# A scheduler that knows one shared port: a new order of work for an FFT, maxout and SoLU kernel on one Trainium2 core

## The chip, the cores and the metric

The kernel runs on one core of one Trainium2 chip. The core has five engines that work side by side, each through its own list of instructions in order: TensorE (PE, matrix products), VectorE (DVE), ScalarE (ACT), GpSimd (POOL) and SyncE (SP), which here only starts transfers (DMA). SBUF is the on-chip memory that all of them read and write; PSUM is a smaller one in which matrix products land. The metric is device time in microseconds (us), the median of several executions.

## The reference

The program is a two-dimensional FFT of which the real part is kept, then a maxout layer of three branches, then a SoLU layer with a normalisation:

```python
def reference(x, w1, w2, w3, w_out, w_in, w_out2, g_ln):     # x (8, 3072, 256)
    X = np.fft.fft(np.fft.fft(x, axis=1), axis=2).real
    X = X.reshape(8 * 3072, 256)
    a = np.maximum(np.maximum(X @ w1, X @ w2), X @ w3)        # 256 -> 768
    y = a @ w_out                                             # 768 -> 256
    h = y @ w_in                                              # 256 -> 1024
    e = np.exp(h - h.max(-1, keepdims=True))
    solu = h * e / (e.sum(-1, keepdims=True) + 1e-09)
    mu = solu.mean(-1, keepdims=True)
    var = ((solu - mu) ** 2).mean(-1, keepdims=True)
    return ((solu - mu) / np.sqrt(var + 1e-06) * g_ln) @ w_out2   # 1024 -> 256
```

Inputs come as 64-bit floats, the output has 24576 rows.

## The kernel before

**Tiling.** The eight batch blocks are worked through in 48 steps, six per block, each of 512 output rows. The first FFT axis is split in two matrix stages, alpha (once per block) and beta (once per step); the second axis is folded into the weights w1, w2, w3. Values go through PE as pairs of 16-bit numbers, a high part and a low part: a float32 value is cast by ACT to the high part, and GpSimd or DVE subtracts that from the value to get the low part. So for nearly each tile that PE reads there is a GpSimd subtraction ahead of it.

**One step.** Six column chunks (j) with three branches (i). `l1` (L635, PE) makes a branch, with a small beta stage (L530) ahead; ACT (L348) and DVE (L655, L668, L669) finish it; `rl` (L674, DVE) takes the maximum of two branches; `rh` (L678, ACT) and `rlo` (L683, GpSimd) split the result; `m` (L693, PE) multiplies by w_out. `mh` (ACT) and `ml` (L708, GpSimd) split the layer's result `mo`. Then for each of four row tiles `h` (L757, PE), max, exp and scale (L766, L781, L787), `vh` (L814, ACT) and `vl` (L818, GpSimd), a transposing transfer `vt`, and `o` (L832, PE), the product that is written out. Every sixth step, the last of a block, is "special": it has columns of its own, and there the operation of L674 reads two tiles in SBUF, where otherwise one of them lies in PSUM.

**Per block.** x is loaded in four chunks (`xla`, SP), folded by GpSimd (`xgh` L391, `xfly` L433; for block 0 `xgh` is on DVE), squared and split (`xlo` L453, GpSimd, for two chunks of block 0 DVE), and goes into the alpha stage (L471).

**Preparation.** All weights are 64-bit floats in memory. Each is loaded, and DVE turns it into float32 in four instructions (`gd`: L920, L921, L922, L924). The keys are 0, 1, 2 for w3, w1, w2, "o" for w_out, "i" for w_in and "f" for w_out2. Then come a product of the maxout weights with a small DFT matrix `cw` (`t3` and others, L949, L1040), column means of w_out2 (`wfg`, `wfm` L1190, evacuated at L1196), scales by powers of two, and the split in two 16-bit parts (`wil` L1152 for w_in, `wfl` L1220 for w_out2, GpSimd). An operation without instructions, `open` (L1248), comes after all of them; it frees the staging memory for the second layer's tiles, and the first `mh` and so the first `h` depend on it.

**What sets the order.** Nothing of the order is written by hand. Every operation is entered with its engine, a planned duration, the operations it depends on, the buffers it takes and gives, and a due time `vt` (its step, plus a number out of the table `BIAS`, chosen by the operation's name). `Schedule.run` (L250 to L298) then plays through all of them: on each engine it picks, among those that are ready, the one with the smallest pair of (planned start, `vt`), and issues it. So `vt` decides only among operations whose planned start is the same, mostly those that are overdue:

```python
start = max(t, clock[e], *slots)
rank = (max(start, clock[e] + WINDOW[e]), o.vt)
```

`t` is when its inputs are there by plan, `clock[e]` when the engine is free, `slots` when its buffers are. Before, an operation of DVE and one of GpSimd never stand in each other's way in the plan. The order in which the operations are picked is the order of the instructions; synchronisation between engines follows from the data.

Of the kernel before, what the change touches and what calls it, by code (L numbers as in the profile page):

```python
# [37 lines left out]
BIAS = {("xla", 0): 0.924, ("xgh", 0): 24.733, ("xfly", 0): -34.959, ("xsq", 0): 23.794, ("xhi", 0): 18.256,  # L38
        ("xlo", 0): 43.224, ("al", 0): -20.409, ("ah", 0): -7.066, ("alo", 0): -5.301, ("xnm", 0): -16.397,
        ("et", 0): 10.126, ("eth", 0): 11.602, ("etl", 0): -1.123, ("xall", 0): -57.851, ("xsc", 0): -81.962,  # L40
        ("mu", 0): 35.938, "me": -11.444, ("xla", 1): 43.853, ("xgh", 1): -9.882, ("xfly", 1): 12.887,
        ("xsq", 1): 35.589, ("xnm", 1): 32.13, ("xhi", 1): 5.917, ("xlo", 1): -2.706, ("al", 1): 24.31,
        ("ah", 1): 55.437, ("alo", 1): -1.992, ("et", 1): -13.139, ("eth", 1): 18.708, ("etl", 1): -53.13,
        ("xall", 1): -9.436, ("xsc", 1): 2.727, ("mu", 1): -25.808, "xla": -22.81, "xgh": 14.031, "xfly": 106.202,
        "xsq": 141.101, "xnm": 50.062, "xhi": -125.469, "xlo": -81.762, "al": -51.099, "ah": -51.867, "alo": -83.921,
        "et": 0.82, "eth": -4.092, "etl": 0.528, "xall": -54.121, "xsc": -112.086, "mu": 57.404, ("zt", 0): -213.614,
# [20 lines left out]
        ("hf", 47): -63.857, ("os", 47): -15.846, ("const",): -15.666, ("eye",): 16.242, ("constb",): 36.614,  # L67
        ("ld", 0): -17.433, ("ga", 0): 38.059, ("gd", 0): 30.168, ("ld", 1): -15.261, ("ga", 1): -13.662,
        ("gd", 1): 59.201, ("ld", 2): 4.852, ("ga", 2): 6.298, ("gd", 2): -5.654, ("sub", 1): 13.65, ("wc", 1): -40.109,
        ("wce", 1): 17.154, ("am", 1): 20.687, ("wcn", 1): -31.697, ("wne", 1): -17.143, ("wz", 1): 2.591,  # L70
        ("sub", 2): 22.562, ("wc", 2): 39.057, ("wce", 2): 28.715, ("am", 2): -4.123, ("wcn", 2): -24.335,
        ("wne", 2): 37.237, ("wz", 2): -1.79, ("amj",): -17.563, ("ws", "dg"): -46.074, ("ws", "all"): 62.73,
        ("ws", "pow"): 28.767, ("wsc", "part"): 27.98, ("wsc",): 0.287, ("whi", 1): 12.259, ("wlo", 1): -20.428,
# [6 lines left out]
        ("os3", "pow"): 5.53, ("scm", "part"): 47.065, ("scm",): 14.959, ("w3r",): -22.549, ("onm", 0): 11.885,  # L80
        ("ohi", 0): -28.778, ("olo", 0): -3.288, ("onm", 1): -28.401, ("ohi", 1): 25.284, ("olo", 1): -42.867,
        ("w3h",): -49.383, ("w3l",): 23.3, ("ld", "i"): -22.156, ("ga", "i"): 10.736, ("gd", "i"): -26.392,
        ("ami", 0): 19.079, ("wio", 0): 30.795, ("wih", 0): 30.94, ("wil", 0): -27.978, ("ami", 1): -4.217,
        ("wio", 1): 7.182, ("wih", 1): -22.224, ("wil", 1): -6.045, ("amij",): 7.196, ("is", "dg"): 68.428,
        ("is", "all"): 17.003, ("is", "pow"): -4.68, ("isc",): -28.442, ("win",): -7.163, ("gl",): -42.898,
# [5 lines left out]
        ("wf",): 18.981, ("open",): -14.816}  # L91
WINDOW = dict(PE=0, DVE=0, ACT=270, Pool=140, SP=470)
SAME = dict(PE=0, DVE=127, ACT=143, Pool=115, SP=0)


def _trig(num, den):
    num = np.asarray(num) % den
# [1193 lines left out]
```

## Time and profile before

| | us |
|---|---|
| median of three runs | 2072.81 (2070.89 to 2076.14) |
| span of the profiled execution | 2071.3 |
| PE busy in it | 1967.6 (95%) |
| DVE busy | 1731.4 (84%) |
| ACT busy | 1487.6 (72%) |
| POOL busy | 1355.7 (65%) |

The profiled execution's span lies within the range of the three runs, 1.5 us under their median. "Busy" counts an instruction from its start to its end, also when it stands still in between because another engine keeps it from memory. The rows further down are of five kinds: a table by stage (busy time per engine), groups of instructions by line (their sum, the mean of one in ns, and the idle time before them with what ended it), waits of an engine, and a timeline (start, duration, engine, line, operation, tiles; in brackets the idle time just before it and who ended that).

### The profile page before, as it was taken

Reading aid. Unit: us, or ns where it says so; the run is one execution under the profiler, and the core shown is the slowest. Engines: PE = TensorE matmul, PEld = TensorE weight load, DVE = VectorE, ACT = ScalarE, POOL = GpSimd, SP = SyncE. Lnnn points to the kernel's source line nnn. Section 1 sums busy time; section 2 is a strip of 40 time slices with the busy share of each in tenths; the row PEclk is TensorE's granted clock in tenths of the full one; section 3 lists DMA queues with packets and bytes.
Section 4 is the critical chain, followed back from the end, with each engine's and each line's share of the span. In section 5 each row is a group of like instructions: output and inputs, shape, how many; then the busy total and the mean of one; then the engine's idle time right before and its main releaser. Section 6 shows DMA issues by size and latency. Waiting matters only on the chain.

```text
span 2071.3 us, 41047 instructions
## 1 busy us (share of the span) xinstructions
PE 1967.6 (95%) x14892; PEld 1339.3 (65%) x14892; DVE 1731.4 (84%) x3894; ACT 1487.6 (72%) x2933; POOL 1355.7 (65%) x1630
## 2 busy tenths in 40 slices
PE   4659999999999999999999999999999999999998
PEld 2535676666666766666666766676667666666666
DVE  6688889888898879888798888888888888888884
ACT  3668866787668866797677876787667766767765
POOL 4479965696657956597566956576555655655663
PEclk8769999999999999999999999999999999999999
DMA  6624533363344533345334633333433333333335
GB/s 212 154 77 92 120 69 73 60 139 79 67 79 95 113 77 67 83 95 111 72 67 78 118 77 72 72 73 72 82 58 82 72 72 67 72 72 77 62 62 112
DMA packets 472701, 178.82 MB, mean 86 GB/s; under 512 B 453577, under 2 KB 453802, under 8 KB 469290
## 3 DMA queue, kind: packets, MB, share of 16 engines
q1 hardware_dynamic: 472498, 176.20, 40.7%
q8 instruction: 116, 1.90, 0.4%
q14 instruction: 87, 0.71, 0.1%
HBM read 37.75 MB, written 25.17 MB: 30 GB/s over the span
## 4 chain that ended last, share of the span: by engine, by line
PE 73%; DVE 12%; ACT 7%; issue 4%; POOL 2%; DMA 1%; SPq 0%; DVEq 0%; ACTq 0%; POOLq 0%
PE omm L832 19%; PE h L757 19%; PE l L635 17%; PE m L693 15%; DVE l L655 2%; DVE sv L674 2%; DVE v L787 1%; PE beta L530 1%; DVE hst L766 1%; PE alpha L471 1%; ACT jk L792 1%; ACT bs L348 1%; DVE sv L669 1%; ACT e L781 1%; ACT rhl L678 1%
## 5 line engine op out<-in xcount | busy, mean ns | idle before, releaser
L832 PE MATMUL omm<-wf,vt 128*128 128x256 f16 x4608 | 535.2, 273 | 4.7 <-DMA vt<-vh 4.7
L757 PE MATMUL h<-win,mo 128*128 128x512 f16 x2280 | 523.5, 379 | 6.0 <-DVE v L787 4.8
L683 POOL TENSOR_TENSOR rhl<-sv,rhl 128x512 f16<-128x512 f32 x288 | 334.8, 1167 | 269.8 <-ACT rhl L678 258.3
L832 PEld LDWEIGHTS <-vt 128*128 128x128 f16 x4608 | 451.2, 98 | 82.1 <-DMA vt<-vh 5.6
L635 PE MATMUL l<-pq,wl 128*128 128x256 f16 (+2 forms) x3456 | 447.9, 273 | 37.6 <-DVE sv L669 20.5
L818 POOL TENSOR_TENSOR vh<-v,vh 128x1024 f16<-128x1024 f32 x188 | 402.5, 2141 | 73.4 <-ACT vh L814 69.7
L655 DVE SCALAR_TENSOR_TENSOR l<-ny,wn,l 128x256 f32<-128x256 f32 (+1 forms) x672 | 316.7, 482 | 131.8 <-ACT bs L348 129.9
L635 PEld LDWEIGHTS <-wl 128*128 128x128 f16 x3456 | 328.9, 97 | 141.1 <-DVE sv L669 30.6
L693 PE MATMUL m<-rhl,wo 128*128 128x512 f16 x1728 | 417.0, 381 | 1.8 <-POOL wo L1098 1.3
L348 ACT ACTIVATE bs<-l 128x256 f32<-128x256 f32 (+1 forms) x672 | 246.6, 379 | 197.9 <-PE l L635 185.0
L757 PEld LDWEIGHTS <-mo 128*128 128x128 f16 x2304 | 222.9, 98 | 247.9 <-DVE v L787 9.8
L792 ACT ACTIVATE jk<-v,hst 128x1024 f16<-128x1024 f32 x192 | 220.4, 1148 | 96.5 <-DVE v L787 96.2
L766 DVE TENSOR_REDUCE hst<-h 128x1 f32<-128x1024 f32 x190 | 231.2, 1217 | 61.5 <-PE h L757 60.8
L787 DVE SCALAR_TENSOR_TENSOR v<-h,hst,e 128x1024 f32<-128x1024 f32 x190 | 243.2, 1280 | 40.3 <-ACT e L781 31.4
L693 PEld LDWEIGHTS <-wo 128*128 128x128 f16 x1728 | 163.7, 98 | 156.7 <-issue 2.7
L678 ACT CAST rhl<-sv 128x512 f16<-128x512 f32 x288 | 176.2, 613 | 81.1 <-DVE sv L674 59.5
L781 ACT ACTIVATE e<-h,hst,xb 128x1024 f32<-128x1024 f32 x190 | 228.9, 1205 | 6.3
L814 ACT CAST vh<-v 128x1024 f16<-128x1024 f32 x192 | 199.6, 1039 | 2.8 <-DMA vt<-vh 2.8
L674 DVE SCALAR_TENSOR_TENSOR sv<-l,sv 128x512 f32<-128x512 f32 x240 | 164.5, 685 | 2.4
L805 POOL TENSOR_SCALAR hst<-hst,sc 128x1 f32<-128x1 f32 x192 | 66.3, 345 | 139.9 <-ACT jk L792 131.5
L708 POOL TENSOR_TENSOR mo<-s,mw 128x512 f16<-128x512 f32 x96 | 121.7, 1276 | 32.7 <-ACT mw L348 31.9
L668 DVE SCALAR_TENSOR_TENSOR sv<-l,bs 128x256 f32<-128x256 f32 x288 | 120.2, 418 | 8.7 <-POOL bs L647 1.6
(153 smaller groups left out, 2342.5 us busy)
## 6 DMA issues: line engine op xcount, KB each, us to landing
xs<-in_x_dram SPq DMA_DIRECT2D x32, 768.0 KB, 5.5
out_dram<-ob SPq DMA_DIRECT2D x96, 256.0 KB, 2.0
raw<-in_w_dram SPq DMA_DIRECT2D x6, 768.0 KB, 7.4
raw<-in_w_out_dram SPq DMA_DIRECT2D x14, 256.0 KB, 2.9
vt<-vh SPq DMA_TRANSPOSE x192, 4.3
raw<-in_w_in_dram SPq DMA_DIRECT2D x4, 512.0 KB
cb<-in_c_beta_dram SPq DMA_DIRECT2D x1, 1553.0 KB
z<-x SPq DMA_TRANSPOSE x48, 3.5
```

The source lines that it names most:

```text
L348: act.activation(dst, src, AF.Copy, scale=scale)
L635: mm(o, w_[w], hl[:, a, e, c0:c0 + n_], start=(n == 0), stop=(n == 2))
L655: dve.scalar_tensor_tensor(p[:, 0:WA], pq[s][1][:, 0:WA], w, p[:, 0:WA], ALU.mult, ALU.add)
L683: pool.tensor_tensor(t[:, 1], svs.pop((s, j, 0)), t[:, 0], ALU.subtract)
L693: mm(m[:, h], wo[:, w, j, hs], t[:, a], start=(j == 0 and n == 0), stop=(j == NJF - 1 and n == 2))
L757: mm(hp[:, f], m[:, a, d, ts_], win[:, w, d, fs], start=(n == 0), stop=(n == 5))
L766: dve.tensor_reduce(st[:, 0], y["h"], op=ALU.max, axis=AX.XY, negate=True)
L781: act.activation(y["e"], y["h"], AF.Exp, bias=st[:, 11], scale=xbt[s // NSB][:, 12:13], accum_out=st[:, 3])
L787: dve.scalar_tensor_tensor(y["v"], y["h"], st[:, 2], y["e"], ALU.mult, ALU.mult, accum_out=st[:, 4])
L792: act.activation(new(hpool[0], "jk", [128, 2, 512], F16), y["v"], AF.Square, bias=st[:, 4], scale=-float(FF2), accum_out=st[:, 6])
L818: engine.tensor_tensor(y["vh"][:, 1], y["v"].rearrange("p a b -> p (a b)"), y["vh"][:, 0], ALU.subtract)
L832: mm(y["o"][:, 0:D], vt[:, a * 8 + c], wf[:, w, c], start=(n == 0), stop=(n == 23))
```

## The change

The scheduler gets one more rule. Some operations are said to hold a port to SBUF that DVE and GpSimd share: all of GpSimd with a planned duration above 200 ns, and on DVE the four decode instructions, the low-part subtractions, the folding of x, three scale operations, and the maximum of special steps. Such an operation starts, in the plan, no earlier than the last such operation of the other engine ends. Nothing of this is in the program that runs: there is no new wait and no lock in it, and no instruction is added or taken out. The whole `BIAS` table is replaced. Before, its numbers lie within about 230 of zero, now within about 1320; they are on the scale of nanoseconds against the due times of the steps. Two of the some 300 entries are shown. Durations, engines, buffers, and the tables `HOP`, `WINDOW`, `SAME` and `CAPACITY` stay. Lines of the kernel's body move down by 20.

```diff
-        ("wf",): 18.981, ("open",): -14.816}
+        ("wfl", 0): 895.994, ("wfn", 1): -295.076, ("wfh", 1): -1028.944, ("wfl", 1): -145.614, ("wf",): -54.258,
+        ("open",): 1077.592}
...
+PORT = {"gd", "wlo", "w3l", "vl", "xgh", "xlo"}
+
+
+def _holds_port(key, eng, dur):
+    if eng == "Pool":
+        return dur > 200
+    if eng != "DVE":
+        return False
+    if isinstance(key[0], str) and key[0] == "os3":
+        return key[-1] != 0
+    return key[0] in PORT or (key[0] == "rl" and key[1] % NSB == NSB - 1)
...
         self.deps, self.take, self.give, self.lag = list(deps), list(take), list(give), lag
+        self.port = _holds_port(key, eng, dur)
...
         at = {}
+        busy = dict(DVE=0.0, Pool=0.0)
...
                     start = max(t, clock[e], *slots)
+                    if o.port:
+                        start = max(start, busy["Pool" if e == "DVE" else "DVE"])
                     rank = (max(start, clock[e] + WINDOW[e]), o.vt)
...
             clock[o.eng] = end
+            if o.port:
+                busy[o.eng] = end
             o.fn(*o.args)
```

Three places in the order of instructions follow, before and after. Names: `xs`, `uv`, `uh`, `xb` belong to the x of a block, `win` is w_in, `wf` is w_out2, `rhl` the split maximum, `mo` the split result of the maxout layer, `st` a staged weight and `raw` its 64-bit form.

**GpSimd, up to the two `mo` subtractions of step 0**, which are what the first `h` waits for. Before:

```order
L396 MEMSET xb 32x4
L391 TENSOR_TENSOR xs<-xs 96x4x256
L683 TENSOR_TENSOR rhl<-sv,rhl 128x512 x2
L420 TENSOR_SCALAR xb<-xb,sc 128x1 x2
L453 TENSOR_TENSOR uh<-uv,uh 96x1024
L1152 TENSOR_TENSOR win<-st,win 128x512 x2
L683 TENSOR_TENSOR rhl<-sv,rhl 128x512 x2
L1152 TENSOR_TENSOR win<-st,win 128x512 x2
L683 TENSOR_TENSOR rhl<-sv,rhl 128x512
L433 TENSOR_TENSOR uv<-xs 96x512 x2
L708 TENSOR_TENSOR mo<-s_877,mw 128x512
L708 TENSOR_TENSOR mo<-s_976,mw 128x512
```

After:

```order
L440 TENSOR_SCALAR xb<-xb,sc 128x1
L453 TENSOR_TENSOR uv<-xs 97x512 x2
L1240 TENSOR_TENSOR wf<-st,wf 128x1024
L416 MEMSET xb 32x4
L1240 TENSOR_TENSOR wf<-st,wf 128x1024
L703 TENSOR_TENSOR rhl<-sv,rhl 128x512
L411 TENSOR_TENSOR xs<-xs 96x4x256
L703 TENSOR_TENSOR rhl<-sv,rhl 128x512
L453 TENSOR_TENSOR uv<-xs 96x512 x2
L703 TENSOR_TENSOR rhl<-sv,rhl 128x512
L728 TENSOR_TENSOR mo<-s_884,mw 128x512
L728 TENSOR_TENSOR mo<-s_957,mw 128x512
```

Over the whole stretch ahead of these two, sixteen x operations of block 1 have gone behind them (5 of L391, 8 of L433, 3 of L453), with one of L683 and one of L420; none has come ahead of them. The last weight split there is now that of w_out2, before it was that of w_in.

**DVE, around the 128x2 scale operation** (L345, after L365), the place where the second of the two late weights is decoded. Before:

```order
L342 TENSOR_SCALAR am<-am 128x2
L674 SCALAR_TENSOR_TENSOR sv<-l_700,sv 128x512
L920 TENSOR_SCALAR st<-st 128x512
L345 TENSOR_SCALAR am<-am 128x2
L655 SCALAR_TENSOR_TENSOR l_735<-ny,wn,l_735 128x256
L921 TENSOR_SCALAR st<-st 128x512
L979 RECIPROCAL sc<-am 128x1
L922 SCALAR_TENSOR_TENSOR st<-raw,st 128x512
L979 RECIPROCAL sc<-am 128x1
L924 SCALAR_TENSOR_TENSOR st<-raw,st 128x512
L920 TENSOR_SCALAR st<-st 128x512
```

After:

```order
L391 TENSOR_REDUCE am<-spread 128x2
L942 SCALAR_TENSOR_TENSOR st<-raw,st 128x512
L362 TENSOR_SCALAR am<-am 128x2
L371 SCALAR_TENSOR_TENSOR pq<-beta,pq 128x256
L944 SCALAR_TENSOR_TENSOR st<-raw,st 128x512
L365 TENSOR_SCALAR am<-am 128x2
L940 TENSOR_SCALAR st<-st 128x512
L999 RECIPROCAL sc<-am 128x1
L941 TENSOR_SCALAR st<-st 128x512
L999 RECIPROCAL sc<-am 128x1
```

Before, the decode here is that of w_in, between `l1` work of step 0 (`sv`, `l`); after, it is that of w_out2, ahead of that work, and w_in has been decoded earlier.

**SP, the first loads.** `raw` is a 64-bit weight, `xs` a chunk of x, `cw` the DFT matrix, `cal` the alpha matrix, `gl` the gain g_ln. Before:

```order
L878 DMA cal<-in_c_alpha_dram 97x577
L1176 DMA gl<-in_g_ln_dram 128x8x1
L904 DMA raw<-in_w_dram 128x1536 x2
L881 DMA cw<-in_c_w_dram 128x514
L384 DMA xs<-in_x_dram 96x2048
L386 DMA xs<-in_x_last_dram 1x2048
L904 DMA raw<-in_w_dram 128x1536 x2
L384 DMA xs<-in_x_dram 96x2048
L904 DMA raw<-in_w_dram 128x1536
```

After:

```order
L898 DMA cal<-in_c_alpha_dram 97x577
L924 DMA raw<-in_w_dram 128x1536 x2
L404 DMA xs<-in_x_dram 96x2048
L406 DMA xs<-in_x_last_dram 1x2048
L924 DMA raw<-in_w_dram 128x1536 x2
L404 DMA xs<-in_x_dram 96x2048
L1196 DMA gl<-in_g_ln_dram 128x8x1
L901 DMA cw<-in_c_w_dram 128x514
L924 DMA raw<-in_w_dram 128x1536
```

`cw` moved from behind two weight transfers to behind four and two chunks of x.

## Rows read from the trace of the kernel before

**Rows 1.** By stage: us, busy (count) of PE, PEld, DVE, ACT, POOL, clock, DMA, GB/s.

```profile
0.00:170.00 170.00, 95.80 (x585) 64.34 (x586) 124.09 (x222) 97.61 (x185) 97.98 (x71) 0.77 0.49 136
170.00:330.00 160.00, 152.44 (x1132) 101.97 (x1131) 142.00 (x327) 124.03 (x244) 127.97 (x151) 1.00 0.45 95
330.00:2030.00 1700.00, 1685.31 (x12932) 1148.40 (x12931) 1447.99 (x3317) 1245.37 (x2469) 1120.75 (x1391) 1.00 0.40 80
2030.00:2071.30 41.30, 34.02 (x249) 24.62 (x247) 17.31 (x30) 20.56 (x36) 8.98 (x19) 0.95 0.60 120
```

**Rows 2.** Groups of PE, 0 to 170 us: busy, mean ns | idle before, releasers.

```profile
L635 PE MATMUL l<-pq,wl 128*128 128x256 f16 x132 | 20.9, 304 | 25.5 <-DVE sv L669 12.5 <-DVE sv L674 8.6 <-DVE xb L415 2.6
L1040 PE MATMUL prep<-cw,st 128*128 128x256 f32 x24 | 8.6, 520 | 17.1 <-DMA cw<-in_c_w_dram 15.3 <-DVE st L924 1.7
```

**Rows 3.** Groups of DVE, 0 to 170 us: the decode of the weights.

```profile
L920 DVE TENSOR_SCALAR st<-st 128x768 f32<-128x768 f32 (+1 forms) x16 | 16.8, 1053 | 21.7 <-ACT st L916 21.6
L922 DVE SCALAR_TENSOR_TENSOR st<-raw,st 128x768 int32<-128x768 int32 (+1 forms) x16 | 16.3, 1018 | 0.3
L924 DVE SCALAR_TENSOR_TENSOR st<-raw,st 128x768 int32<-128x768 int32 (+1 forms) x16 | 15.7, 980 | 0.3
L921 DVE TENSOR_SCALAR st<-st 128x768 int32<-128x768 int32 (+1 forms) x16 | 12.9, 808 | 0.4
```

**Rows 4.** Timeline of DVE, POOL and PE between 81 and 126 us.

```profile
81.60 0.54 DVE L920 TENSOR_SCALAR st<-st 128x768 f32<-128x768 f32 x1
...
83.76 0.96 DVE L924 SCALAR_TENSOR_TENSOR st<-raw,st 128x768 int32<-128x768 int32 x1
...
110.75 1.83 DVE L920 TENSOR_SCALAR st<-st 128x512 f32<-128x512 f32 x1
...
112.50 3.77 DVE L345 TENSOR_SCALAR am<-am 128x2 int32<-128x2 int32 x1
...
113.91 2.33 POOL L391 TENSOR_TENSOR xs<-xs 96x1024 f32<-96x1024 f32 x1
...
121.00 0.41 DVE L920 TENSOR_SCALAR st<-st 128x512 f32<-128x512 f32 x1
...
122.65 0.68 DVE L924 SCALAR_TENSOR_TENSOR st<-raw,st 128x512 int32<-128x512 int32 x1
...
124.62 1.46 PE L635 MATMUL l<-pq,wl 128*128 128x256 f16 x6 [12.31 <-DVE sv L669]
```

**Rows 5.** Timeline: DFT of the weights, w_out2's chain, and the first h.

```profile
48.99 4.21 PE L949 MATMUL prep<-st,cw 128*128 128x384 f32 x6 [6.25 <-POOL st L943]
...
85.43 0.37 ACT L1196 COPY mean<-prep 128x256 f32<-128x256 f32 x1 [3.95 <-PE prep L1190]
...
108.08 4.21 POOL L1220 TENSOR_TENSOR wf<-st,wf 128x1024 f16<-128x1024 f32 x2 [0.93 <-ACT wf L1216]
...
169.54 1.24 PE L757 MATMUL h<-win,mo 128*128 128x512 f16 x5
```

**Rows 6.** Groups of POOL, 0 to 170 us: the x work.

```profile
L433 POOL TENSOR_TENSOR uv<-xs 96x512 f32<-96x512 f32 (+1 forms) x20 | 27.3, 1385 | 18.6 <-DVE xs L391 18.3
L391 POOL TENSOR_TENSOR xs<-xs 96x1024 f32<-96x1024 f32 (+1 forms) x7 | 16.6, 2377 | 0.7 <-DMA xs<-in_x_dram 0.6
L453 POOL TENSOR_TENSOR uh<-uv,uh 96x1024 f16<-96x1024 f32 (+1 forms) x5 | 11.9, 2375 | 10.9 <-ACT uh L445 7.7 <-DVE st L921 3.2
```

**Rows 7.** Special steps, 330 to 2030 us: a group, one case, PE's waits.

```profile
L674 DVE SCALAR_TENSOR_TENSOR sv<-sw,sv 128x512 f32<-128x512 f32 x43 | 52.4, 1219 | 0.5
...
1272.41 2.13 POOL L818 TENSOR_TENSOR vh<-v,vh 128x1024 f16<-128x1024 f32 x1 [1.41 <-ACT vh L814]
1272.45 2.64 DVE L674 SCALAR_TENSOR_TENSOR sv<-sw,sv 128x512 f32<-128x512 f32 x1
...
PE l L635 <- DVE sv L669: 5.7, 11, 1.7
```

**Rows 8.** Timeline of PE in the last 20 us.

```profile
2060.85 6.81 PE L832 MATMUL omm<-wf,vt 128*128 128x256 f16 x48 [3.28 <-DMA vt<-vh]
```

More of the change, by code (lines that the diff above doesn't have):

```diff
@@ L37 @@
 HOP = dict(PE=200, DVE=130, ACT=150, Pool=150, SP=60)
[L38 to L46, printed above, removed]
[20 rows of a table removed]
[L67 to L73, printed above, removed]
[6 rows of a table removed]
[L80 to L85, printed above, removed]
-        ("ld", "f"): -43.368, ("ga", "f"): 6.612, ("gd", "f"): 10.13, ("wfg", 0): -13.295, ("wfg", 1): -3.645,
-        ("wfg", 2): -9.739, ("wfg", 3): 5.268, ("wfm",): 21.588, ("wfe",): -36.028, ("wfs", 0): 66.321,
-        ("amf", 0): -22.861, ("wfs", 1): -10.945, ("amf", 1): 23.161, ("amfj",): 59.432, ("fs", "dg"): -30.537,
-        ("fs", "all"): 7.01, ("fs", "pow"): -47.813, ("wfc", "part"): 19.001, ("wfc",): -25.835, ("wfn", 0): 18.746,
-        ("wfh", 0): 26.324, ("wfl", 0): 8.648, ("wfn", 1): -13.905, ("wfh", 1): 18.869, ("wfl", 1): -9.387,
-        ("wf",): 18.981, ("open",): -14.816}
@@ new lines @@
+BIAS = {("xla", 0): -329.39, ("xgh", 0): -352.9, ("xfly", 0): -237.583, ("xsq", 0): -435.605, ("xhi", 0): -107.549,
+        ("xlo", 0): -1322.849, ("al", 0): -257.121, ("ah", 0): -372.322, ("alo", 0): -843.063, ("xnm", 0): -438.913,
+        ("et", 0): -26.783, ("eth", 0): -472.589, ("etl", 0): 21.7, ("xall", 0): -231.403, ("xsc", 0): -762.511,
+        ("mu", 0): -263.605, "me": -989.32, ("xla", 1): 812.734, ("xgh", 1): 1087.32, ("xfly", 1): -706.162, ("xsq",
+        1): -784.131, ("xnm", 1): 273.605, ("xhi", 1): -41.517, ("xlo", 1): -296.985, ("al", 1): -59.039, ("ah", 1):
+        23.429, ("alo", 1): -1245.312, ("et", 1): 41.852, ("eth", 1): -787.021, ("etl", 1): -37.623, ("xall", 1):
+        -671.872, ("xsc", 1): 150.998, ("mu", 1): -146.585, "xla": -121.712, "xgh": 860.482, "xfly": 104.414, "xsq":
+        88.716, "xnm": 825.803, "xhi": -264.459, "xlo": -876.228, "al": -887.438, "ah": -103.593, "alo": 758.005,
+        "et": -792.112, "eth": -676.383, "etl": -484.142, "xall": -422.562, "xsc": 925.06, "mu": -227.338, ("zt", 0):
[23 rows of a table added]
+        902.054, ("sub", 1): -353.424, ("wc", 1): -74.322, ("wce", 1): -904.275, ("am", 1): -349.423, ("wcn", 1):
+        -613.95, ("wne", 1): 476.473, ("wz", 1): 607.37, ("sub", 2): 21.812, ("wc", 2): -1099.738, ("wce", 2):
+        -124.669, ("am", 2): -326.155, ("wcn", 2): 1085.624, ("wne", 2): -1047.421, ("wz", 2): -742.007, ("amj",):
+        756.246, ("ws", "dg"): -870.362, ("ws", "all"): -257.833, ("ws", "pow"): 252.253, ("wsc", "part"): 519.632,
+        ("wsc",): 757.111, ("whi", 1): -475.846, ("wlo", 1): -288.588, ("whi", 2): -203.12, ("wlo", 2): 606.608,
[6 rows of a table added]
+        -197.78, ("scm",): -789.692, ("w3r",): -199.777, ("onm", 0): -992.761, ("ohi", 0): -889.296, ("olo", 0):
+        -842.891, ("onm", 1): -281.679, ("ohi", 1): 617.645, ("olo", 1): -203.121, ("w3h",): -904.114, ("w3l",):
+        -251.361, ("ld", "i"): -1239.52, ("ga", "i"): -671.925, ("gd", "i"): -269.314, ("ami", 0): 353.278, ("wio",
+        0): -576.076, ("wih", 0): -996.473, ("wil", 0): -266.625, ("ami", 1): -789.095, ("wio", 1): -368.532, ("wih",
+        1): -890.573, ("wil", 1): 704.53, ("amij",): -109.604, ("is", "dg"): -540.108, ("is", "all"): 6.052, ("is",
+        "pow"): -660.953, ("isc",): 73.116, ("win",): -922.531, ("gl",): -312.41, ("ld", "f"): 151.409, ("ga", "f"):
+        -381.267, ("gd", "f"): -978.057, ("wfg", 0): 1084.436, ("wfg", 1): 16.262, ("wfg", 2): -400.13, ("wfg", 3):
+        -82.377, ("wfm",): 151.873, ("wfe",): -53.124, ("wfs", 0): -519.032, ("amf", 0): 718.226, ("wfs", 1):
+        -908.005, ("amf", 1): -1080.261, ("amfj",): -666.536, ("fs", "dg"): 79.961, ("fs", "all"): 723.361, ("fs",
+        "pow"): -308.223, ("wfc", "part"): 837.499, ("wfc",): -501.014, ("wfn", 0): -290.121, ("wfh", 0): -842.554,
+        ("wfl", 0): 895.994, ("wfn", 1): -295.076, ("wfh", 1): -1028.944, ("wfl", 1): -145.614, ("wf",): -54.258,
+        ("open",): 1077.592}
```

55 rows, old and new, of the table BIAS are left out of this document.

## The prediction

> **What bounds the kernel now.** First the table by stage, for where PE is not at work [rows 1]. Span less busy time of PE is 74.2 us in the first 170 us (170 − 95.8), 7.6 up to 330, 14.7 in the 1700 us after that, and 7.3 in the last 41. In the steady part PE is 99% busy at full clock. The order of work can't shorten PE's own work, so of the 2071.3 us only these 103.8 are at stake, and 74 of them lie ahead of the first `h`, which starts at 169.54 [rows 5].
>
> Second, the groups of PE in that stretch, for what it waits on. Idle ahead of L635 is 25.5 us, 12.5 of it for DVE's `sv` [rows 2], and one wait makes up nearly all of that: 12.31 us at 124.62 [rows 4].
>
> Third, DVE there. The decode of the weights is 64 instructions, together 16.8 + 16.3 + 15.7 + 12.9 = 61.7 us [rows 3]. Undisturbed they take less: a 768-wide one 0.54 us in the first form (L920) and 0.96 in the second (L924), a 512-wide one 0.41 and 0.68 [rows 4]. Each form is two of the four lines and half the weights have each width, so free time would be 8 × (2 × 0.54 + 2 × 0.96) + 8 × (2 × 0.41 + 2 × 0.68) = 24.0 + 17.4 = 41.4 us. That is 20.3 us of stretching. One instruction on two numbers per partition (L345, 112.50) took 3.77 us, where a 512-wide one takes 0.41: at least 3.4 more. So DVE stands still for about 23.7 us here. It does so beside GpSimd's work: the 1.83 us decode of 110.75 lies beside the `wf` split of 108.08 to 112.29 [rows 5], and the 3.77 us one ended at 116.27, 0.03 us after the x fold that GpSimd began at 113.91 [rows 4]. The lock of the change is about this. It exists in the plan alone: what can change is which instructions stand side by side.
>
> **The change part by part.** *Up to the first `h`, what moves behind it.* GpSimd drops 5 of L391, 8 of L433 and 3 of L453 from in front of the two `mo` subtractions: 5 × 2.38 + 8 × 1.39 + 3 × 2.38 = 30.1 us [rows 6], all x work of block 1, not needed before step 6. Nothing new comes ahead. On PE, small pieces of block 1 and of step 1 go behind too, 11 operations and by the same rows' kind about 6.2 us; that is work put off, not saved.
>
> *What is then late.* `open` waits for the last weight. Before, w_in came last: decoded from 110.75 on, its split and the x work on GpSimd then lay in front of `mo`. After, w_in is decoded early and w_out2 comes last. Its chain took from the evacuation of its means at 85.43 to the end of its last split at 112.29, 26.9 us [rows 5]. In the new order its mean product stands behind `l1` of chunk 3 of step 0; counting PE's work and waits in front of it by the trace of before gives an end at 115 to 120 (estimate). Plus 26.9, plus some 4 to 5 for the `mo` split: first `h` at 146 to 152, 18 to 23 us sooner. Less the 6.2 us of PE work put off, PE loses 12 to 17 us fewer. The bounds: nothing gained (the chain through w_out2 is as late as that through w_in was) and 23.7 (all of DVE's standing still). I take **−14**, near the one row that shows such a stall, 12.31.
>
> *The first loads.* `cw` goes behind two more weight transfers and two chunks of x on SP. PE waited 15.3 us for it [rows 2], so `t3` starts 10 to 15 us later. Behind it PE waits 6.25 us for a GpSimd subtraction at 48.99 anyway [rows 5], and only 95.8 of 170 us are work, so it can be caught up; 0 to 2 us, contained in the −14. Uncovered it would cost 15 − 6.25 = 9 us; that keeps the upper end.
>
> *Steps 0 to 5.* The 30.1 us on GpSimd come back. From 170 to 330 it was busy 128.0 of 160 us [rows 1], so 32 us are free, enough in sum. By the order, 22 of the 30 stand in front of the `vl` of the third tile of step 2; by step 4 both orders have the same work behind them. PE then waits when a split comes late. Bounds: −3 (the x work in step 0 was in the way too) and +27.5 (rival C). PE was held up 7.6 us in all in this stretch, with GpSimd 80% busy; I take **+4**, near that row.
>
> *Special steps.* From 330 to 2030 the 43 maxima of L674 with both inputs in SBUF took 52.4 us [rows 7]; another instruction with two 512-wide inputs takes 0.68 [rows 4], so 43 × 0.68 = 29 us of work and 23 us of standing still on DVE, a good part of it hidden: PE waits 5.7 us there for `sv` (11 waits) [rows 7]. Bounds −5.7 and +5.7; the new order keeps these apart by plan, but one case shows how little of the plan need be off: GpSimd began at 1272.41 and DVE at 1272.45, and the maximum took 2.64 us [rows 7]. I take **−3**.
>
> The Trainium skill ("SBUF — State Buffer", sections on the two sides of SBUF and "Who interferes with whom") says that the pair of ports is locked by whichever engine starts first, for that whole instruction, and that the order of issue, not the shape, decides who waits. The case at 1272.41 agrees (0.04 us decide 2 us); the one at 112.50 doesn't quite, since there DVE was issued 1.41 us ahead of the fold and still ended after it. Taken strictly, the rule speaks against this change: a plan can't promise 0.04 us, so special steps would give 0 for −3, and the sum would be 3 us higher.
>
> *The end.* PE waits 3.28 us at 2060.85 for the transposed tile [rows 8]; the new order puts the last product of step 46 and the first of 47 in another sequence, with one more product in front of that place. Bounds −3.3 and +3.3, taken **−2**.
>
> Everything else is the same instructions on the same engines, so it costs nothing, with PE's 99% in the steady part as the cover; if due times there were worse, it would show as PE's idle time above 14.7.
>
> Sum: 2071.3 − 14 + 4 − 3 − 2 = 2056.3 us of span; the median lay 1.5 above the span of before, so **2058**.
>
> **The rivals.** *B, the start gains nothing (the change doesn't do what it says).* Instructions drift by more than 0.04 us against the plan, so the decode of w_out2 meets other GpSimd work, as that of w_in did, and the new last chain takes 18 to 23 us longer than 26.9. For it: it is a chain over DVE, ACT, GpSimd and PE, each step with a hop, and 23.7 us of stretching moved to it are just that gap. Against it: 16 GpSimd instructions that were the partners of the stretch are gone from there. Time: 2071.3 + 0 − 3 − 2 + 1.5 = 2068, with the 5.7 and 3.3 either way 2063 to 2076.
>
> *C, GpSimd's backlog in steps 0 to 2 (slower).* Its idle time of 32 us lies in pieces, behind the casts that it waits for, and can't be filled. If it stays 20% idle with 22 us more to do, the 160 us become (128 + 22) / 0.8 = 187.5: +27.5, PE waiting for `vl` and `rlo`. Time: 2071.3 − 14 + 27.5 − 2 + 1.5 = 2084. It turns the sign from a backlog cost of some 19 us on, that is when GpSimd keeps nearly its whole idle share. Against it: what was moved is only wanted in step 6, and the subtractions in question have due times of their own, ahead of it.
>
> **How the numbers follow.** The main case: 0.64, 2042 to 2067. B: 0.22, 2063 to 2076. C: 0.14, 2077 to 2090. In the main case all at its best would be 2071.3 − 23.7 − 3 − 5.7 − 3.3 + 1.5 = 2037; I leave 0.06 below 2042. With C left out above 2078 (0.13) the range is 2042 to 2078. 0.3% is 6.2 us, about what a measurement of this kernel can tell from no change: faster is below 2066.6, slower above 2079. Faster 0.61 of the main case and 0.06 of B: 0.67. Same: 0.03, 0.16 and 0.01 of C: 0.20. Slower: 0.13.
>
> **What would show it.** In the profile after: first `h` (L777) between 146 and 152 us; PE's idle time up to it about 60 in place of 74; the 64 decodes together nearer 45 than 61.7 us; the wait for `sv` at L655 in the start gone. Between first `h` and step 3, PE's idle time at about 12 in place of 7.6, with GpSimd over 85% busy there. The special maxima at a mean nearer 0.9 than 1.22 us. Wrong would make it: a first `h` behind 160 (B); PE idle over 20 us between first `h` and 330, released by GpSimd (C); `t3` so late that the first beta stage is late with it; or waits at L852 for the transposed tile all through the steady part, since the new due times let some `h` and `o` of one tile come closer together.

## The result

The changed kernel took 2043.13 us (median of four runs, 2041.56 to 2043.93), the kernel before, beside it, 2074.19 (2070.89 to 2076.14). The ratio is 0.9856, with a 95% interval of 0.9842 to 0.9869: some 31 us faster, where 15 were forecast. The time lies within the stated range of 2042 to 2078, 1 us from its lower end. The profiled execution spans 2042.1 us, 29.2 less than that of before.

The table by stage, cut at the first `h`, answers to [rows 1]; columns are us, then busy time and count of PE, PE's weight loads, DVE, ACT and GpSimd, granted clock, DMA share, GB/s:

```profile
0.00:85.00 85.00, 41.41 (x234) 31.19 (x235) 62.94 (x85) 45.04 (x82) 30.69 (x26) 0.80 0.61 177
85.00:142.28 57.28, 43.48 (x256) 28.07 (x255) 44.87 (x118) 40.26 (x84) 37.36 (x29) 0.88 0.35 95
142.28:330.00 187.72, 182.84 (x1408) 123.28 (x1406) 167.87 (x391) 152.25 (x297) 167.89 (x188) 1.00 0.49 108
330.00:2000.00 1670.00, 1656.59 (x12722) 1131.77 (x12721) 1425.49 (x3269) 1226.76 (x2431) 1100.42 (x1368) 1.00 0.40 80
2000.00:2042.10 42.10, 36.21 (x279) 26.75 (x277) 19.16 (x34) 24.05 (x42) 16.24 (x22) 0.99 0.62 126
```

PE's idle time up to the first `h` is now (85 − 41.41) + (57.28 − 43.48) = 57.4 us, before 74.2. Behind it 4.9, 13.4 and 5.9, before 7.6, 14.7 and 7.3 [rows 1]. GpSimd is 89% busy from the first `h` to 330 (before 80%), and PE waits less there, not more.

The 29.2 us in full: idle up to the first `h` −16.8, in the 188 us behind it −2.7, in the steady part −1.3, at the end −1.4, and PE's busy time −7.0 (1967.6 to 1960.5 by the page).

The groups of PE and of DVE up to 170 us answer to [rows 2] and [rows 3]:

```profile
L655 PE MATMUL l<-pq,wl 128*128 128x256 f16 x179 | 26.8, 297 | 10.3 <-DVE sv L694 4.8 <-DVE sv L689 2.7 <-DVE s L689 1.7
L1060 PE MATMUL prep<-cw,st 128*128 128x256 f32 x24 | 8.5, 525 | 28.7 <-DMA cw<-in_c_w_dram 28.5
```

```profile
L944 DVE SCALAR_TENSOR_TENSOR st<-raw,st 128x768 int32<-128x768 int32 (+1 forms) x16 | 16.0, 998 | 0.3
L940 DVE TENSOR_SCALAR st<-st 128x768 f32<-128x768 f32 (+1 forms) x16 | 14.2, 886 | 16.0 <-ACT st L936 15.9
L942 DVE SCALAR_TENSOR_TENSOR st<-raw,st 128x768 int32<-128x768 int32 (+1 forms) x16 | 14.1, 881 | 0.2
L941 DVE TENSOR_SCALAR st<-st 128x768 int32<-128x768 int32 (+1 forms) x16 | 10.2, 639 | 0.3
```

The wait of 12.3 us is gone (the longest for `sv` in the start is now 1.7); the 64 decodes take 54.5 us, before 61.7. Their free time, that is without a neighbour that holds them up, is 41.4 us by the prediction's count. The timeline of DVE (answers to [rows 4]) shows where the 13 us of stretching that are left lie:

```profile
40.33 3.38 DVE L940 TENSOR_SCALAR st<-st 128x768 f32<-128x768 f32 x1
...
55.96 2.05 DVE L940 TENSOR_SCALAR st<-st 128x512 f32<-128x512 f32 x1 [0.23 <-ACT st L936]
58.04 0.43 DVE L941 TENSOR_SCALAR st<-st 128x512 int32<-128x512 int32 x1
58.51 0.69 DVE L942 SCALAR_TENSOR_TENSOR st<-raw,st 128x512 int32<-128x512 int32 x1
```

They lie ahead of 58 us, where GpSimd folds the x of block 0 and subtracts weights, work that is needed there. Behind 58 us nearly all decodes take their free time: of the stretching, 12.6 us lie ahead of 58 us and 0.4 behind, in before 9.2 and 11.0. So what the new order has removed is the stretching of the late weights. And the way to the first `h` (PE and GpSimd, answers to [rows 5]):

```profile
105.79 1.13 PE L1210 MATMUL prep<-st,ones 128*128 128x256 f32 x4 [1.01 <-ACT st L368]
...
129.05 2.13 POOL L1240 TENSOR_TENSOR wf<-st,wf 128x1024 f16<-128x1024 f32 x1 [0.18 <-ACT wf L1236]
131.18 1.15 POOL L703 TENSOR_TENSOR rhl<-sv,rhl 128x512 f16<-128x512 f32 x1
132.29 2.35 POOL L411 TENSOR_TENSOR xs<-xs 96x1024 f32<-96x1024 f32 x1
134.61 1.15 POOL L703 TENSOR_TENSOR rhl<-sv,rhl 128x512 f16<-128x512 f32 x1
135.72 2.50 POOL L453 TENSOR_TENSOR uv<-xs 96x512 f32<-96x512 f32 x2
138.19 1.16 POOL L703 TENSOR_TENSOR rhl<-sv,rhl 128x512 f16<-128x512 f32 x1
139.31 2.49 POOL L728 TENSOR_TENSOR mo<-s,mw 128x512 f16<-128x512 f32 x2
...
142.28 2.75 PE L777 MATMUL h<-win,mo 128*128 128x512 f16 x12
```

The chain through w_out2 is what the prediction named, and GpSimd stands without a gap between its last split and `mo`.

### The profile page after: what moved, and what is told of

Same layout as the page of the kernel before. It is cut to its first block, busy times and chain, and to the rows that moved or that the text cites. A ratio compares the mean times of both kernels' runs of the same rounds, so it can differ in the third digit from the quotient of the medians.

```text
span 2042.1 us, 40722 instructions
## 1 busy us (share of the span) xinstructions
PE 1960.5 (96%) x14892; PEld 1341.1 (66%) x14892; DVE 1720.3 (84%) x3894; ACT 1488.4 (73%) x2933; POOL 1352.6 (66%) x1630
## 4 chain that ended last, share of the span: by engine, by line
PE 66%; DVE 8%; ACT 8%; POOL 5%; issue 3%; DMA 1%; DVEq 0%; POOLq 0%; ACTq 0%
PE h L777 17%; PE omm L852 17%; PE l L655 15%; PE m L713 13%; DVE v L807 2%; ACT jk L812 2%; POOL vh L838 2%; DVE hst L786 1%; ACT e L801 1%; PE beta L550 1%; PE alpha L491 1%; DVE l L675 1%; DVE sv L694 1%; DMA vt<-vh 1%; POOL rhl L703 1%
## 5 line engine op out<-in xcount | busy, mean ns | idle before, releaser
L655 PEld LDWEIGHTS <-wl 128*128 128x128 f16 x3456 | 329.6, 97 | 121.4 <-DVE sv L689 16.8
L713 PEld LDWEIGHTS <-wo 128*128 128x128 f16 x1728 | 168.1, 98 | 164.8 <-issue 3.8
L807 DVE SCALAR_TENSOR_TENSOR v<-h,hst,e 128x1024 f32<-128x1024 f32 x190 | 243.5, 1281 | 29.8 <-ACT e L801 15.3
L859 ACT ACTIVATE ob<-omm,hst 128x256 f32<-128x256 f32 x192 | 89.8, 468 | 69.6 <-PE omm L852 49.4
```

The source lines that it names most:

```text
L655: mm(o, w_[w], hl[:, a, e, c0:c0 + n_], start=(n == 0), stop=(n == 2))
L713: mm(m[:, h], wo[:, w, j, hs], t[:, a], start=(j == 0 and n == 0), stop=(j == NJF - 1 and n == 2))
L807: dve.scalar_tensor_tensor(y["v"], y["h"], st[:, 2], y["e"], ALU.mult, ALU.mult, accum_out=st[:, 4])
```

## The experiments

Theory: the gain lies ahead of the first `h`, and it is GpSimd's work in company with the decode (side by side with it) that was in the way. Rivals: GpSimd's queue alone, that is the x work standing in front of `mo`; the order of the weights; the lock as such, the table as such; and, behind the first `h`, GpSimd's backlog. The edits are shortened: `...` stands for what is left out, and words behind # are remarks. The numbers in one table first. Each ratio is taken against executions of before beside it, whose median lay between 2072.1 and 2074.2. Idle time is PE's, span less busy time by stage: up to the first `h`, in the 187.7 us behind it, from there to 2000, and after. First `h`, idle and busy time are of one execution each. new_start, lock_start_only, old_rest_locked and no_special_lock issue the same instructions in the same order as after up to the first `h`, so their first `h` at 140.5 to 142.3 and their 57.4 to 59.8 us of idle time up to it show how far two executions can lie apart.

| kernel | time, ratio to before (interval) | first h | idle by stage | PE busy |
|---|---|---|---|---|
| before | 2074.19 | 169.5 | 74.2, 7.6, 14.7, 7.3 | 1967.6 |
| after | 2043.13, 0.9856 | 142.3 | 57.4, 4.9, 13.4, 5.9 | 1960.5 |
| lock_old_table | 2102.19, 1.0146 (1.0131 to 1.0161) | 206.5 | 99.0, 3.1, 11.7, 12.4 | 1974.7 |
| new_table_no_lock | 2072.70, 1.0001 (0.9992 to 1.0011) | 168.9 | 73.5, 9.6, 11.4, 9.9 | 1968.6 |
| x_held | 2091.86, 1.0098 (1.0082 to 1.0114) | 150.6 | 62.6, 30.5, 13.6, 8.4 | 1972.8 |
| company_add | 2058.29, 0.9933 (0.9916 to 0.9949) | 157.0 | 73.0, 4.9, 13.5, 6.0 | 1959.8 |
| company_fill | 2048.70, 0.9881 (0.9866 to 0.9895) | 146.1 | 62.7, 4.9, 13.7, 6.1 | 1959.1 |
| cw_first | 2044.32, 0.9859 (0.9845 to 0.9874) | 143.1 | 56.8, 4.9, 13.7, 6.0 | 1962.1 |
| new_start | 2086.77, 1.0063 (1.0048 to 1.0078) | 140.5 | 58.5, 15.3, 32.6, 8.3 | 1968.7 |
| new_rest | 2059.42, 0.9935 (0.9918 to 0.9951) | 168.7 | 73.7, 6.4, 8.7, 6.5 | 1963.1 |
| x_paced | 2098.95, 1.0125 (1.0110 to 1.0140) | 150.3 | 61.8, 8.4, 44.0, 8.5 | 1975.2 |
| lock_start_only | 2049.50, 0.9885 (0.9870 to 0.9899) | 141.4 | 59.8, 7.0, 11.8, 9.4 | 1959.3 |
| old_rest_locked | 2083.89, 1.0052 (1.0037 to 1.0067) | 141.5 | 59.5, 15.0, 26.9, 12.4 | 1971.2 |
| no_special_lock | 2049.50, 0.9887 (0.9870 to 0.9903) | 140.7 | 58.8, 7.1, 12.1, 9.3 | 1959.9 |

**The port, by itself.** Useless GpSimd work is put where GpSimd waits anyway, the order being that of after:

```diff
+    with_company(("xlo", 0, 1), 4)     # pool.tensor_tensor(dum, dum, dum, ALU.add)
+    with_company(("wz", 2), 5)
+    with_company(("w3z",), 4)
```

> The kernel after in its own order, with 13 additions of 896 columns in SBUF put in on GpSimd where it waits anyway (4 behind xlo of chunk 1 of block 0, 5 behind the second wz, 4 behind w3z): about 27 us of work that nobody needs, beside the weight decode. Theory of the port: DVE stands still beside them, the decode and the weight scaling between 57 and 110 us take 8 to 15 us longer, first h 4 to 12 us later than 142.3, time 2047 to 2056. Rival (only GpSimd's queue in front of mo counts): GpSimd was idle there, first h within 2 us, time 2042 to 2046.

It took 15 us more than after and the first `h` came 14.7 us later: the theory's sign, a larger size than its 4 to 12, and nothing of the rival, by which work in GpSimd's idle time costs nothing. DVE beside GpSimd in its timeline:

```profile
58.13 7.84 POOL L1279 TENSOR_TENSOR dum<-dum 128x896 f32<-128x896 f32 x4
...
58.48 1.78 DVE L943 TENSOR_SCALAR st<-st 128x512 int32<-128x512 int32 x1
60.30 2.05 DVE L944 SCALAR_TENSOR_TENSOR st<-raw,st 128x512 int32<-128x512 int32 x1
62.39 2.05 DVE L946 SCALAR_TENSOR_TENSOR st<-raw,st 128x512 int32<-128x512 int32 x1
```

Four additions in 7.84 us, 1.96 each, and beside them each DVE instruction takes about as long (1.78 to 2.05), whatever its free time (0.43 and 0.69 in after at the same place): one addition goes by for one DVE instruction. The decode, all of it:

```profile
L946 DVE SCALAR_TENSOR_TENSOR st<-raw,st 128x768 int32<-128x768 int32 (+1 forms) x16 | 18.7, 1168 | 0.3
L944 DVE SCALAR_TENSOR_TENSOR st<-raw,st 128x768 int32<-128x768 int32 (+1 forms) x16 | 17.6, 1100 | 0.2
L942 DVE TENSOR_SCALAR st<-st 128x768 f32<-128x768 f32 (+1 forms) x16 | 17.3, 1084 | 16.2 <-ACT st L938 16.0
L943 DVE TENSOR_SCALAR st<-st 128x768 int32<-128x768 int32 (+1 forms) x16 | 14.2, 889 | 0.3
```

67.8 us, 13.3 more than after. To tell the port from GpSimd's being busy, fills take the additions' place:

```diff
+    with_company(("xlo", 0, 1), 9)     # pool.memset(dum, 0.0)
+    with_company(("wz", 2), 11)
+    with_company(("w3z",), 9)
```

> As company_add, at the same three places of GpSimd's list, but with 29 fills of 896 columns (0.845 us each in the run with additions, 24.5 us together; the 13 additions took 24.7) that write SBUF and read nothing. If GpSimd's being busy there is what cost the 15 us (its own later work comes late), the time is 2054 to 2060 as with the additions. If it is the port and only GpSimd's reading holds it against DVE operations with two SBUF inputs, the forms with two inputs (L944, L946 lines by after) keep 0.68 and 0.96, and the time is 2043 to 2048; if the fills hold it as well, each DVE operation beside them takes 0.85 and the time lies between, near 2050.

GpSimd was busy as long (29 fills took 26.6 us, 13 additions 24.7), and 5.6 us were lost in place of 15.2. The time lies 0.7 us above the 2043 to 2048 that were expected if only GpSimd's reading counts. Its timeline:

```profile
57.67 8.82 POOL L1279 MEMSET dum<- 128x896 f32 x9
...
58.05 1.03 DVE L943 TENSOR_SCALAR st<-st 128x512 int32<-128x512 int32 x1
59.11 0.69 DVE L944 SCALAR_TENSOR_TENSOR st<-raw,st 128x512 int32<-128x512 int32 x1
59.84 0.69 DVE L946 SCALAR_TENSOR_TENSOR st<-raw,st 128x512 int32<-128x512 int32 x1
```

The forms with two inputs in SBUF keep 0.69 beside fills; the form with one input goes from 0.43 to 1.03. So some 60% of the price of the additions (9.6 of 15.2 us) is due to what GpSimd reads, not to its being busy; and the other 5.6 us aren't all its being busy, since the one-input form is held up by fills too. The Trainium skill ("SBUF — State Buffer", sections "SBUF: two separate sides" and "Who interferes with whom") says of the two-input operations that they meet GpSimd only where it reads SBUF, and of `tensor_scalar`, the one-input form here, that it can run in a mode that takes the shared pair of ports and then contends with GpSimd; the runs agree on both (0.69 and 1.03 us beside fills).

**Lock or table.** First the lock with the table of before:

```diff
-BIAS = {("xla", 0): -329.39, ...          # the new table
+BIAS = {("xla", 0): 0.924, ...            # the table of before
```

> The scheduler's lock with the table of before. In this order 31 x operations (L411, L453 by the after lines) stand ahead of the first mo subtraction on GpSimd, where before has 22 and after 9. Theory (what counts is how much GpSimd work lies in front of and beside the weight decode): first h later than the 169.5 us of before, 172 to 190, and a time of 2073 to 2095. Rival (the lock itself is the gain, the table only trims it): first h near 150 and a time of 2045 to 2060.

The theory's side, worse than its range: first `h` at 206.5, 30 us slower than the before beside it. A plan that reckons with the port is not faster by itself. Then the table without the lock:

```diff
-                    if o.port:
-                        start = max(start, busy["Pool" if e == "DVE" else "DVE"])
```

> The new table without the lock. 11 x operations ahead of the first mo subtraction (after 9). Theory (the order of the start does it, whoever made it): first h at 142 to 150, time 2043 to 2055. Rival (the lock does it): the decode lies beside GpSimd work again, first h at 160 or later, time above 2060.

No change against before, so here the rival was right on the time, but not for its reason. The decode is not stretched more than in after, and DVE waits for what it is to decode:

```profile
L942 DVE SCALAR_TENSOR_TENSOR st<-raw,st 128x768 int32<-128x768 int32 (+1 forms) x16 | 15.0, 939 | 0.3
L940 DVE SCALAR_TENSOR_TENSOR st<-raw,st 128x768 int32<-128x768 int32 (+1 forms) x16 | 15.0, 938 | 0.3
L938 DVE TENSOR_SCALAR st<-st 128x768 f32<-128x768 f32 (+1 forms) x16 | 11.8, 738 | 27.1 <-ACT st L934 27.1
L939 DVE TENSOR_SCALAR st<-st 128x768 int32<-128x768 int32 (+1 forms) x16 | 11.2, 699 | 0.3
```

53.0 us of decode, but 27.1 of waiting (after 16.0), and the last decode ends at 123.7 in place of 105.2: one load of w_in went out at 87.92, after the last of them at 60.00. Few x operations ahead of `mo` are not enough; the loads and decodes have to come in time as well. That the table was chosen for a plan with the lock's starts would explain why it needs them, but that isn't shown. Its numbers aren't nanoseconds: they are added as they are to a due time in steps, which spans only some 50. Of the new table's 255 numbers 238 are over 50 in size (before 78 of 283), so it mostly ranks kinds of operations, whatever their step.

**Is it the moved x work?** The kernel before, with one dependency more:

```diff
-        op(("xgh", *k), ..., v - 0.3, deps=[("xla", *k)])
+        op(("xgh", *k), ..., v - 0.3, deps=[("xla", *k)] + [("ml", 0, 1)] * (b == 1))
```

> The kernel before with one more dependency: the x work of block 1 on GpSimd may start only behind the second mo subtraction of step 0, so that 6 x operations stand ahead of the first mo (before 22). Weight order, table and plan otherwise as before, no lock. Theory: the wait of 12.3 us for sv is gone, the 64 decodes take 50 to 56 us in place of 61.7, first h at 145 to 155, time 2050 to 2060. Rival (the new order of the weights, w_in first and w_out2 last, is the gain): first h at 163 or later and a time of 2066 to 2075.

The first `h` came at 150.6, 19 us sooner, without table, lock or a new order of weights, as the theory had it. Not as the theory had it, the longest wait for `sv` is still 7.0 us and the decode takes 58.9, where 50 to 56 were expected. So company isn't all of it. In before, GpSimd's own list was in the way as well: it is busy for 35.3 of the 37.8 us from 130.33 to the first `mo` subtraction at 168.10, and over half of that is x work of block 1:

```profile
L391 POOL TENSOR_TENSOR xs<-xs 96x1024 f32<-96x1024 f32 (+1 forms) x3 | 7.3, 2419 | 0.1
L453 POOL TENSOR_TENSOR uh<-uv,uh 96x1024 f16<-96x1024 f32 (+1 forms) x3 | 6.4, 2130 | 0.7 <-ACT uh L445 0.7
L433 POOL TENSOR_TENSOR uv<-xs 97x512 f32<-97x512 f32 (+1 forms) x4 | 5.9, 1498 | 0.0
```

company_add and company_fill show that company has a price of its own; x_held takes company and queue away at once, so how the gain of the start divides between them is not shown. The time was 32 us above its range. Everything came back behind the first `h`:

```profile
150.58:330.00 179.42, 150.67 (x1103) 99.76 (x1102) 130.98 (x311) 128.63 (x242) 153.55 (x155) 0.92 0.46 103
```

28.8 us of PE idle time, with GpSimd 86% busy: the size of rival C of the prediction, in another kernel, though only 4.6 us of PE's waits there are ended by GpSimd itself, the most by DVE and ACT. GpSimd's list there has six x instructions between the second `mo` and the first `vl`, and seven more between the first two `vl`. So the chunks were released one step apart (the new end of the line alone):

```diff
+           deps=[("xla", *k)] + [("ml", NSB * (b - 1) + c, 1)] * (b > 0))
```

> The kernel before with the x work of each block spread over the steps of the block ahead: chunk c of block b may be folded only behind the second mo subtraction of step 6(b-1)+c. x_held released four chunks at once behind the first mo and lost 30.5 us of PE idle time in the 187.7 us behind its first h. Theory (that loss is GpSimd's backlog): first h near 150.6 as in x_held, idle time in the 187.7 us behind it at 5 to 12 us, time 2055 to 2068. Rival (it comes from the old order of the weights and of step 0, whatever x does): idle time there above 20 us, time above 2075.

Right on the first `h` (150.3) and on the stretch behind it (8.4 us in place of 30.5), so that loss came of the four chunks released at once. Wrong on the time: PE lost 44.0 us later (some 30 between 290 and 650), waiting for DVE's `sv` and `v` and once 3.2 us for a transposed tile. The dependency makes the scheduler plan all of the rest anew with due times fitted to another flow; which of them fails there wasn't followed.

**The first load.** In after's order, `cw` issued first:

```diff
     const_load()
+    const_load2()
-    pop(("const",), "SP", 750, const_load2, (), -0.85, lag=2000)
+    pop(("const",), "SP", 750, lambda: None, (), -0.85, lag=2000)
```

> The kernel after with the load of cw issued first on SP; all else stays in its order. The DFT products (L1060) can start at about 16 to 20 in place of 28.55 us. Theory (PE has room there, DVE's decode of w1 and w2 and GpSimd set the pace up to 58 us): first h within 2 us of 142.3, time 2041 to 2044. Rival (the 13 us by which the first load came later were a loss): first h 5 to 9 us sooner, time 2034 to 2038.

No gain: the 13 us by which `cw` came later are covered, as the theory had it. The same products of `cw` then wait 28.1 us for other things, 19.0 for DVE's decode and 9.1 for ACT.

**Start and rest apart.** The scheduler switches table and lock once the first `h` is planned (new_rest the other way round):

```diff
-                    if o.port:
+                    if o.port and not begun:
...
+            if k == ("h", 0, 0):
+                begun = True
+                for m in self.ops.values():
+                    m.vt = m.late          # due time by the other table
```

> The scheduler runs with the lock and the new table until the first h has been planned, and from there on with the table of before and without the lock. Theory (the gain lies ahead of the first h): first h at 142 to 143, time 2043 to 2052, special maxima back to a mean of 1.1 to 1.25 us. Rival (the new order in steps 0 to 5 keeps the gain from being given back): PE's idle time from the first h to 330 us over 10 us, time 2055 to 2070.

> The other half: table of before and no lock until the first h has been planned, from there on the new table with the lock. Theory: first h at 169 to 170, special maxima at a mean of 0.75, time 2066 to 2073. Rival (the lock is worth something in the steady part): 2058 to 2065.

Both theories fell; of new_rest, the rival's time of 2058 to 2065 was met. The new start with the old rest is slower than before by 13 us, although its first `h` comes at 140.5. PE's idle time behind it:

```profile
140.48:330.00 189.52, 174.20 (x1271) 113.98 (x1269) 150.95 (x355) 139.03 (x268) 154.01 (x174) 0.97 0.44 89
330.00:2000.00 1670.00, 1637.41 (x12614) 1119.47 (x12612) 1412.87 (x3235) 1214.28 (x2406) 1095.80 (x1333) 1.00 0.40 80
```

15.3 and 32.6 us. And the new rest with the old start saves 14 us, with the first `h` at 168.7. So the two halves don't add: new start alone +13, new rest alone −14, both −31. Behind the new start the new rest is worth 44 us (2086.8 to 2043.1), behind the old one 14. Next, which part of the rest:

```diff
-                    if o.port:
+                    if o.port and not begun:       # lock until the first h, new table all through
```

> The new table all through, the lock only until the first h has been planned. Theory (behind the first h the table's due times carry the gain and the lock moves only DVE's own waiting): first h at 140 to 143, special maxima back at 1.0 to 1.25 us, time 2042 to 2050. Rival (the lock is needed behind the first h as well): PE idle behind the first h above 35 us (24.2 in the kernel after), time 2055 to 2085.

```diff
-                    if o.port and not begun:       # of new_start
+                    if o.port:                     # lock all through, old table behind the first h
```

> New table until the first h has been planned, the old one behind it, the lock all through. new_start, which is the same without the lock behind the first h, took 2086.8 with 56 us of PE idle time behind it. If the lock is what keeps the rest in order, idle time behind the first h falls to 24 to 32 us and the time to 2045 to 2060; if the table is, it stays at 2075 to 2095.

```diff
-    return key[0] in PORT or (key[0] == "rl" and key[1] % NSB == NSB - 1)
+    return key[0] in PORT
```

> The kernel after, but the maximum of special steps isn't said to hold the port; all other holders stay. Theory (what DVE stands still there is mostly hidden): special maxima at a mean of 1.0 to 1.25 us in place of 0.75, PE's idle time from 330 to 2000 up by 0 to 6 us from 13.4, time 2042 to 2050. Rival (these waits are on PE's path): idle time up by over 10 us, time above 2053.

The table is it: with it and no lock behind the first `h` the time is 2049.5, with the lock and the old table 2083.9. The lock saves some 6 us there, about the size that can be told, and all of that by the entry of the special maxima, since without that entry the time is the same 2049.5 and GpSimd's list is the same as without the lock. It isn't saved where most of the maxima are: with the lock PE's idle time in the table's third stretch is 1.6 us more, and 2.1 and 3.5 less in the second and the last (after against lock_start_only). The expected size of those maxima was wrong: 0.78 us in both (41 in 330 to 2000 us), where 1.0 to 1.25 was expected. The table without the lock and the lock without the table each keep them nearly clear of GpSimd, where the maxima of before take 1.22 [rows 7] (new_table_no_lock, then lock_old_table, 330 to 2000 us):

```profile
L692 DVE SCALAR_TENSOR_TENSOR sv<-sw,sv 128x512 f32<-128x512 f32 x39 | 29.3, 752 | 0.4
L693 DVE SCALAR_TENSOR_TENSOR sv<-sw,sv 128x512 f32<-128x512 f32 x42 | 33.2, 789 | 0.4
```

## Why the prediction was right, and where it wasn't

The sign, the place of most of the gain and the mechanism at the start were right; the size was half of what was measured, and the range held by 1 us. Of the 29.2 us, 7.0 are in PE's busy time, for which the prediction had no term, and the near hit of the start is in part luck. By its terms:

- **The start, −14: measured −16.8.** The way there was less exact than the sum. w_out2's mean product ended at 106.9, forecast 115 to 120; its chain took 24.3 us (forecast 26.9); and from its last split to the first `h` it took 11.1 us, forecast 4 to 5, because six GpSimd instructions, three of them x work of block 1, still stood ahead of `mo` (the rows at 131.18 to 138.19). Against the middle of the forecast, 149, the product was put some 10.6 us too late, the chain 2.6 too long and the last piece 6.6 too short; they made 142.3, outside "146 to 152", and that errors of both signs left the term near is luck. The decode got less free than forecast (54.5 us, not near 45), since the remaining stretch is beside block 0's own x work. That GpSimd's company stretches the decode and delays the first `h` is shown (company_add, company_fill); that moving x work behind `mo` is by itself enough for a first `h` some 19 us sooner too (x_held). The prediction named both the x work in front of `mo` and its company with the decode and didn't price them apart; the runs don't either, so how the 16.8 us divide is open.
- **The first loads, 0 to 2 with 9 uncovered: nothing.** PE waited 28.5 us in place of 15.3 for `cw`, and cw_first gained nothing.
- **Steps 0 to 5, +4: measured −2.7.** This is the step that failed most on reasoning: it took GpSimd's load of 80% and added work to it, as if the order of the rest stayed. A loss of the size that it feared is real: 30.5 us in x_held, near the 27.5 of rival C. In new_start it is 15.3, but there none of PE's longer waits is ended by GpSimd, so that this one is a backlog is not shown. In after there is no such loss, with GpSimd 89% busy, and by new_start, old_rest_locked and lock_start_only (15.3, 15.0 and 7.0 us) it is above all the new table that keeps it away, not the lock. Which of its entries does so is open.
- **Special steps, −3: measured −1.3 in the whole steady part.** The group shows DVE's standing still nearly gone, as forecast and more:

```profile
L694 DVE SCALAR_TENSOR_TENSOR sv<-sw,sv 128x512 f32<-128x512 f32 x42 | 31.4, 748 | 0.6
```

1.22 us each before [rows 7], 0.75 now, 20 us of DVE's time in all; PE's idle time fell by 1.3, so it was hidden. The doubt drawn from the order of issue (a plan can't promise 0.04 us) did not come true: the maxima got shorter, and nearly all of that comes by the table or by the lock, either alone (0.75 and 0.79). Who waits when two such instructions meet within 0.04 us was not tested by this.
- **The end, −2: measured −1.4.** The wait of 3.28 us [rows 8] is down to 0.53, and one of 1.47 us for ACT's `ob` is new:

```profile
2035.78 2.79 PE L852 MATMUL omm<-wf,vt 128*128 128x256 f16 x24 [0.53 <-DMA vt<-vh]
```

- **"The order of work can't shorten PE's own work": wrong, by 7.0 us.** Matched instruction by instruction, 3.0 us of that are in the weight preparation, 0.8 in block 0's alpha stage, 1.6 in step 0, less 1.3 in step 1 and 0.5 in steps 2 to 5; 3.4 are in steps 6 to 47. PE's clock is a part of the reason in the start. Before, PE did little between 110 and 125 us, and the clock granted there was the lower of its two levels, 1.2 GHz; in after it works on in that stretch (before, then after; the first row has PE alone):

```profile
110.00:125.00 15.00, 1.82 (x8) 0.50 0.14 42
```

```profile
110.00:120.00 10.00, 7.23 (x30) 3.28 (x30) 4.47 (x11) 6.92 (x14) 9.23 (x6) 0.83 0.01 2
```

By the clock granted at each one's start, the matmuls of the first 330 us that had the lower level before and the upper one after take 8.6 us less together, those the other way round 6.8 us more. At the end, before was granted the lower level for 3.4 us from 2060.3 on, as the wait of 3.28 ended, and after only behind its last matmul: that is 1.4 us, in products of step 47. So a changed level makes up some 3.2 of the 7.0 us; the rest, with 1.9 of the 3.4 us of steps 6 to 47, stays unexplained. The kernels taken together agree in direction: those with the most idle time (lock_old_table 126 us, x_paced 123) have the highest PE busy time (1975), those with the least (after 82, cw_first 81) 1960 to 1962; but company_add, with 97 us, has 1960, so idle time alone doesn't set it.

The terms' errors sum to −2.8 − 6.7 + 1.7 + 0.6 − 7.0 = −14.2, from 2056.3 to 2042.1 of span. Rival B (the start gains nothing) did not happen, but it is what new_table_no_lock did, for another reason. The same early start with the old rest ends slower than before, as rival C does (2086.8 and 2084), but with only 15.3 of its 27.5 us in that stretch and more of the loss later.

## What to carry to other kernels

Where GpSimd and DVE work side by side, count what stands beside the long DVE chain that everything waits for: useless additions in GpSimd's own idle time cost 15 us of 2043 here, fills of about the same length 5.6. An earlier start is not yet a gain: four kernels of this study reached the first `h` 19 to 29 us sooner than before and ended 10 to 25 us later than it, since they lost more behind it: x_held because what was put off came back all at once, the other three by waits that weren't followed to their cause. So price the put-off work with the order in which it will come back, not with the engine's load alone. A cost model and the priorities that go with it have to be tested together: here each alone was worth nothing or less.

## What was unexpected of the hardware

Beside GpSimd additions DVE and GpSimd go one for one, so a DVE instruction of 0.43 us took 1.78 and two of 0.69 took 2.05, about the length of the neighbour's (1.96). GpSimd fills don't hold DVE's two-input forms at all (0.69 and 0.69), but do hold its one-input form (0.43 to 1.03).
